# Where the product steps stand among the attention slots of chunks 2 and 3, and which bank turns chunk 3's x

## The chip, the cores and the metric

The kernel runs on one core of one Trainium2 chip. The metric is the device time of one execution in microseconds (us). The engines are named as the profile names them: PE (TensorE) multiplies matrices, PEld is its loading of weights, ACT (ScalarE) applies functions, DVE (VectorE) does elementwise work, POOL (GpSimd) and SP (SyncE) here mainly issue transfers.

## The reference

An attention layer over 4 batches, 8 heads, 768 positions and 64 numbers per head is followed by a two-layer network. Three heads look back over everything, five only at the first 4 positions (the sinks) and the last 64.

```python
scores = q @ k.T / sqrt(64)                    # [4, 8, 768, 768]
keep   = causal if head in (0, 2, 6) else causal & (pos_k < 4 or 0 <= pos_q - pos_k < 64)
a      = softmax(where(keep, scores, -1e9))
x      = (a @ v).transpose(0, 2, 1, 3).reshape(3072, 512)
h      = x @ w_in                              # [3072, 2048]
out    = maximum(0.01 * h, h) @ w_out          # [3072, 512]
```

## The kernel before

**Chunks.** The 3072 rows are cut into eight chunks of 384. `ORDER` runs them as (batch 0, first half), (batch 1, first half), (batch 0, second half), (batch 1, second half), then the same for batches 2 and 3. Chunks 2 and 3 are thus second halves and need six blocks of keys each.

**Attention of a chunk** (`Attention`) is a list of *slots*, made by `slots(lag=3)`. A *unit* is one group of scores and the values that belong to it: five groups for each of the three full heads, one for each of the five windowed heads, and one group for the sinks, 21 units. Slot t issues the scores of unit t (`qk`, L329, for windowed heads L364, for the sinks L309) into a PSUM bank named `psS`, with the exponential on ScalarE behind it (L334, L369, L312) and, where needed, a mask on VectorE (L337, L339, L373). In the same slot come the value matmuls of unit t - 3 (`do_av`, L298, into `po`). Where a pair of heads is complete, `finish` (L395, L397) adds the sinks' values, takes the reciprocal of the sums and writes `xs`. Three slots later `x_t` turns `xs` with three small matmuls against the identity (L407) and copies the result into `xt`, on ScalarE (L409) or on VectorE (L411). Chunks 2 and 3 so have 21 + 3 + 3 = 27 slots: slots 0 to 20 issue scores, slots 21 to 23 only values, slots 24 and 25 nothing, slot 26 the turn of the last pair. From chunk 4 on, `cross` is set, and the turn is a DMA transpose instead.

**The network of a chunk** has two products. Product 1 (`in_slots`, L563) is 16 steps of four 384-column matmuls into a bank `ph`, each with its activation on ScalarE (L565). Product 2 (`out_slots`, L589) is 16 steps, 48 matmuls of 512 columns, into a bank `py`; the steps hold two to four matmuls each. Each third of a chunk keeps one `py` bank until its 16 matmuls are done; then VectorE copies it out (L595) and SP stores it (L596).

**Banks.** The eight PSUM banks are split by `BANKS` into two each of `ph`, `psS`, `po` and `py`. A matmul that writes a bank waits until the engine that read its last content has done so.

**Order.** The schedule is by hand (`manual_schedule`): each engine runs its instructions in the order in which the program issues them. `merge(ms, as_)` spreads the slots `as_` evenly ahead of the product steps `ms`. Three places matter:

- While chunk 2's attention runs, the product steps beside it are the last four of chunk 0's product 2 (`o0[12:]`) and the first ten of chunk 1's (`o1[0:10]`): 14 steps, 42 matmuls, among 27 slots. Then come `spreads(3)` (VectorE copies chunk 3's turned keys into `kt`, L237).
- In the loop at n = 2, chunk 3's attention stands among chunk 2's product 1 and the rest of chunk 1's product 2, 22 steps in all. Chunk 4's key copies (`spreads(4)`, eight of them) go with the slots from the 17th on.
- At the end of n = 2, the last four steps and the last three slots have an order of their own.

Chunk 2's x is turned in a bank `ph` and copied by ScalarE (`xt_tag="ph"`); chunk 3's is turned in a bank `psS`, the default, and copied by VectorE (`xt_eng="v"`).

Of the kernel before, what the change touches and what calls it, by code (L numbers as in the profile page):

```python
# [21 lines left out]
def kernel(  # L22
# [84 lines left out]
    def load_qk(n, nms="kq"):  # L107
        b, c = ORDER[n]
        for nm in nms:
            t = rot.tile([128, 3, H, D], BF16, name=f"{nm}b", tag=f"{nm}b", bufs=1)  # L110
            raw[nm, n] = t
            for g in range(3):
                nc.gpsimd.dma_start(out=t[:, g], in_=nat[nm][b, c, :, :, g])  # L113

    def load_v(n, gs=range(3)):
        b, c = ORDER[n]
        for g in gs:
            nc.gpsimd.dma_start(out=va[b][:, 3 * c + g, :, 0:D], in_=nat["v"][b, c, :, :, g])  # L118
# [3 lines left out]
    def load_sinks(b, eng=None):  # L122
        vsf[b] = rot.tile([32, D], FP32, name="vsf", tag="vsf", bufs=2)
        (eng or nc.sync).dma_start(out=vsf[b][:], in_=v[b, :, 0:NS, :])

    def sink_values(b, eng):
        n = H - 1
        eng.tensor_tensor(
            vs[b % 2][0:32, 1:H, 0:D],
            vsf[b].rearrange("p (o d) -> p o d", o=1).to_broadcast([32, n, D]),  # L130
            m_sink[0:32, 1:H].rearrange("p (h o) -> p h o", o=1).to_broadcast([32, n, D]),
            op=ALU.mult)
# [8 lines left out]
    def v_shift(n, eng=None):  # L141
        eng = eng or nc.sync
        i, c = ORDER[n]
        lo, hi = (0, 2) if c == 0 else (2, 5)
        eng.dma_start(out=vb[i][0:64, lo:hi], in_=va[i][64:128, lo:hi])
        eng.dma_start(out=vb[i][64:128, lo:hi], in_=va[i][0:64, lo + 1 : hi + 1])
# [77 lines left out]
    def turn_dma(n):  # L224
        qx[n] = rot.tile([128, 3, 4, 128], BF16, name="qd", tag="qd", bufs=3)
        raw["kx", n] = rot.tile([128, 3, 4, 128], BF16, name="kd", tag="kd", bufs=2)
        for nm, dst in (("k", raw["kx", n]), ("q", qx[n])):
            nc.sync.dma_start_transpose(out=dst.rearrange("p g q t -> p (g q) t"),
                                        in_=raw[nm, n].rearrange("p g h d -> p (g h d)"))

    def spreads(n):
        b, c = ORDER[n]

        def spread(g, hh):
            r = slice(64 * hh, 64 * hh + 64)
            o = CH * c + 128 * g
            nc.vector.tensor_copy(kt[b % 2][hh][r, :, o : o + 128], raw["kx", n][r, g])  # L237

        r = [lambda g=g, hh=hh: spread(g, hh) for g in range(3) for hh in range(2)]
        if c == 0:  # L240
            r += sink_keys_by(b)
        return r
# [4 lines left out]
    def into(slots, extra):  # L247
        r, extra = [], list(extra)
        for j, s in enumerate(slots):
            r.append(s)  # L250
            if 5 * j >= 2 * len(slots) and extra:
                r.append(extra.pop(0))
                if len(extra) > len(slots) - j - 2:
                    r.append(extra.pop(0))
        return r + extra
# [299 lines left out]
    py = {}  # L555

    def in_slots(n, tags=("ph",)):
        def tick(t):
            if n not in gs:
                gs[n] = rot.tile([128, NG, CH], BF16, name="g", tag="g", bufs=2)  # L560
            ph = bank(tags[t % len(tags)], [128, 512], FP32)
            for g in range(KG):
                nc.tensor.matmul(ph[:, 0:CH], lhsT=w_in_bf[:, g, 128 * t : 128 * t + 128],  # L563
                                 rhs=xts[n][:, g, :] if n else xts[0][:, :, g, :], start=(g == 0), stop=(g == KG - 1))
            nc.scalar.activation(out=gs[n][:, t, :], in_=ph[:, 0:CH], func=ACTF.Prelu, alpha=0.01)  # L565

        return [lambda t=t: tick(t) for t in range(NG)]
# [14 lines left out]
    def out_slots(n, tags=("py", "py", "py"), halves=False):  # L582
        slots = []

        def part(tt, lo, hi, tag, c0, c1):
            if lo == 0:
                py[n] = bank(tag, [128, 512], FP32)
            for ng in range(lo, hi):
                nc.tensor.matmul(py[n][:, 0 : c1 - c0], lhsT=gs[n][:, ng, 128 * tt : 128 * tt + 128],  # L589
                                 rhs=w_out_bf[:, ng, c0:c1], start=(ng == 0), stop=(ng == NG - 1))  # L590
            if hi == NG:
                o = rot.tile([128, DM], FP32, name="o", tag="o", bufs=6)
                b, c = ORDER[n]
                r0 = S * b + CH * c + 128 * tt
                nc.vector.tensor_copy(o[:, 0 : c1 - c0], py[n][:, 0 : c1 - c0])  # L595
                nc.sync.dma_start(out=out[r0 : r0 + 128, c0:c1], in_=o[:, 0 : c1 - c0])  # L596

        for tt in range(3):
            if halves and tt == 2:
                slots.append(lambda: part(2, 0, NG, "py", 0, 256))  # L600
                slots.append(lambda: part(2, 0, NG, "psS", 256, 384))
                slots.append(lambda: part(2, 0, NG, "po", 384, 512))
                continue
            lo = 0
            for w in ([3, 3, 3, 3, 4], [3, 3, 3, 3, 4], [3, 3, 3, 3, 2, 2])[tt]:
                slots.append(lambda tt=tt, lo=lo, w=w: part(tt, lo, lo + w, tags[tt], 0, DM))
                lo += w
        return slots

    def run(*lists):  # L610
        for l in lists:
            for f in l:
                f()

    def both(s, e):
        return lambda: (s(), e and e())

    def merge(ms, as_):

        r, done = [], 0  # L620
        for j, m in enumerate(ms):
            want = (j + 1) * len(as_) // len(ms)
            r += as_[done:want] + [m]
            done = want
        return r + as_[done:]
# [152 lines left out]
    o0, o1 = out_slots(0), out_slots(1)  # L778
# [1 line left out]
    run(spreads(2))  # L780
    run(o0[6:12])
    v_shift(3)
    run(merge(o0[12:] + o1[0:10], Attention(2, xt_tag="ph").slots(lag=3)))
    run(spreads(3))
    outs = o1[10:]

    for n in range(2, NCH):
        a, extra = [], ()
        if n + 2 < NCH:
            turn_dma(n + 2)  # L790
            v_shift(n + 2)
            extra = spreads(n + 2)
            if ORDER[n + 2][1] == 0:
                load_sinks(ORDER[n + 2][0], nc.gpsimd)
                sink_values(ORDER[n + 2][0], nc.gpsimd)
            if n + 3 < NCH:
                load_qk(n + 3)
                load_v(n + 3)
        if n + 1 < NCH:
            a = Attention(n + 1, xt_eng="v", cross=n > 2).slots(lag=2 if n > 2 else 3)  # L800
            a = into(a, extra) if n > 2 else a
        ms = merge(in_slots(n), outs)
        rest = ms[-9:] if a and n > 2 else []
        if n == 2:
            a, rest = [both(s, e) for s, e in zip(a[:-3], [None] * 16 + extra)], [ms[-4], a[-3], ms[-3], a[-2], a[-1], ms[-2], ms[-1]]
            ms = ms[:-4] + rest
        run(merge(ms[: len(ms) - len(rest)], a), rest)
        outs = out_slots(n) if n + 1 < NCH else out_slots(n, ("psS", "psS", "py"), True)
    run(outs)
# [35 lines left out]
```

## Time and profile before

| What | Value |
|---|---|
| Runs | 234.07, 233.84, 235.79, 234.61 us |
| Median | 234.34 us |
| The profiled execution, its own time | 234.07 us |
| Its span in the trace | 232.3 us |
| PE busy | 224.9 us (97%) |
| ACT busy | 127.8 us (55%) |
| DVE busy | 98.3 us (42%) |
| POOL busy | 71.2 us (31%) |
| Granted PE clock, mean | 1.00 |

The span runs from the first instruction to the end of the last; the time of the execution is 1.8 us more. A row of a timeline gives the start in us from the span's start, the length, the engine, the line of the kernel, what it writes and reads, the shape, how many were merged into the row, and in brackets the idle time before it with what ended it. The length of a matmul in these rows holds its way through the array, which overlaps with the next one, so the pace of matmuls is read from the differences of their starts.

### The profile page before, as it was taken

Reading aid. Unit: us, or ns where it says so; the run is one execution under the profiler, and the core shown is the slowest. Engines: PE = TensorE matmul, PEld = TensorE weight load, DVE = VectorE, ACT = ScalarE, POOL = GpSimd, SP = SyncE. Lnnn points to the kernel's source line nnn. Section 1 sums busy time; section 2 is a strip of 40 time slices with the busy share of each in tenths; the row PEclk is TensorE's granted clock in tenths of the full one; section 3 lists DMA queues with packets and bytes.
Section 4 is the critical chain, followed back from the end, with each engine's and each line's share of the span. In section 5 each row is a group of like instructions: output and inputs, shape, how many; then the busy total and the mean of one; then the engine's idle time right before and its main releaser. Section 6 shows DMA issues by size and latency. Waiting matters only on the chain.

```text
span 232.3 us, 5117 instructions
## 1 busy us (share of the span) xinstructions
PE 224.9 (97%) x2080; PEld 139.2 (60%) x2080; DVE 98.3 (42%) x282; ACT 127.8 (55%) x275; POOL 71.2 (31%) x87
## 2 busy tenths in 40 slices
PE   7899999999999999999999999999999999999994
PEld 4687865545655666656566655666555665555554
DVE  7797475042556278367224541245213341111121
ACT  5767856705756875654365536766366764343300
POOL 8996635048068088185006700000000000000000
PEclk9999999999999999999999999999999999999999
DMA  9999999999999999999959992921210220111112
GB/s 132 166 164 181 205 207 164 179 155 173 160 224 202 177 177 143 150 165 169 134 104 176 179 159 65 185 65 34 65 45 0 65 80 20 45 45 45 48 45 92
DMA packets 109480, 28.98 MB, mean 125 GB/s; under 512 B 101248, under 2 KB 105744, under 8 KB 109456
## 3 DMA queue, kind: packets, MB, share of 16 engines
q0 software_dynamic: 77088, 13.39, 76.9%
q1 hardware_dynamic: 31312, 15.00, 30.7%
q10 hardware_dynamic: 1056, 0.26, 0.5%
q8 instruction: 16, 0.26, 0.5%
q14 instruction: 8, 0.07, 0.1%
HBM read 27.30 MB, written 6.29 MB: 145 GB/s over the span
## 4 chain that ended last, share of the span: by engine, by line
PE 86%; POOL 5%; DMA 4%; DVE 3%; issue 0%; ACT 0%; POOLq 0%
PE py L589 31%; PE ph L563 30%; PE po L298 7%; PE psS L329 5%; DMA w_in_bf<-in_moe_w_in_dram 4%; PE psS L589 3%; PE psS L364 3%; PE psS L563 2%; PE psS L309 2%; PE ph L576 1%; POOL kb L113 1%; POOL va L118 1%; POOL qb L113 1%; DVE kt L237 1%; POOL k L104 1%; POOL q L105 1%
## 5 line engine op out<-in xcount | busy, mean ns | idle before, releaser
L589 PE MATMUL py<-w_out_bf,g 128*128 128x512 bf16 (+1 forms) x352 | 90.9, 374 | 0.0
L563 PE MATMUL ph<-xt,w_in_bf 128*128 128x384 bf16 x448 | 90.4, 326 | 0.0
L565 ACT ACTIVATE g<-ph 128x384 bf16<-128x384 f32 x112 | 54.9, 490 | 57.5 <-PE ph L563 56.5
L563 PEld LDWEIGHTS <-w_in_bf 128*128 128x128 bf16 x480 | 44.1, 98 | 31.3
L589 PEld LDWEIGHTS <-g 128*128 128x128 bf16 x416 | 35.9, 98 | 25.8
L334 ACT ACTIVATE at<-psS 128x384 bf16<-128x384 f32 x78 | 36.9, 489 | 18.7 <-PE psS L329 18.5
L595 DVE COPY o<-py 128x512 f32<-128x512 f32 (+1 forms) x22 | 14.9, 679 | 51.3 <-PE py L589 51.0
L113 POOL DMA_DIRECT2D kb<-in_k_dram x21 | 18.7, 908 | 37.6 <-DMA kd<-kb 36.5
L329 PE MATMUL psS<-qd,kt 128*128 128x384 bf16 (+2 forms) x90 | 23.0, 294 | 0.5 <-ACT at L334 0.3
L118 POOL DMA_DIRECT2D va<-in_v_dram x24 | 21.6, 930 | 2.2 <-DMA w_out_bf<-in_moe_w_out_dram 1.8
L113 POOL DMA_DIRECT2D qb<-in_q_dram x21 | 18.6, 915 | 5.7 <-DMA w_in_bf<-in_moe_w_in_dram 1.8
L298 PE MATMUL po<-va,at 128*128 128x65 bf16 x228 | 19.2, 193 | 0.0
L369 ACT ACTIVATE ats<-psS 128x384 bf16<-128x384 f32 x35 | 16.7, 488 | 3.6 <-PE psS L364 3.1
L373 DVE TENSOR_TENSOR ats<-ats,m_win 128x384 bf16<-128x384 bf16 x35 | 12.7, 365 | 14.3 <-ACT ats L369 13.8
L298 PEld LDWEIGHTS <-at 128*128 128x128 bf16 x234 | 14.8, 98 | 4.8 <-issue 0.2
L397 DVE TENSOR_TENSOR xs<-po,linv 128x384 bf16<-128x384 f32 x27 | 15.0, 557 | 0.9
L237 DVE COPY kt<-kd 64x512 bf16<-64x512 bf16 x36 | 14.6, 404 | 0.6
L329 PEld LDWEIGHTS <-kt 128*128 128x128 bf16 x99 | 9.4, 97 | 8.1 <-issue 0.9
L364 PEld LDWEIGHTS <-kt 128*128 128x128 bf16 x210 | 10.6, 98 | 5.4
L339 DVE TENSOR_TENSOR at<-at,m_caus 128x128 bf16<-128x128 bf16 x21 | 4.7, 223 | 21.0 <-ACT at L334 20.8
L298 PEld LDWEIGHTS <-ats 128*128 128x128 bf16 x210 | 10.4, 97 | 4.0 <-DVE xs L397 0.4
L395 DVE RECIPROCAL linv<-po 128x6 f32<-128x6 f32 x27 | 5.2, 193 | 16.1 <-PE po L298 16.0
(143 smaller groups left out, 205.2 us busy)
## 6 DMA issues: line engine op xcount, KB each, us to landing
out_dram<-o SPq DMA_DIRECT2D x23, 256.0 KB, 2.3
va<-in_v_dram POOLq DMA_DIRECT2D x24, 128.0 KB, 7.6
kb<-in_k_dram POOLq DMA_DIRECT2D x21, 128.0 KB, 5.5
qb<-in_q_dram POOLq DMA_DIRECT2D x21, 128.0 KB, 6.2
w_in_bf<-in_moe_w_in_dram POOLq DMA_DIRECT2D x4, 512.0 KB, 8.9
w_out_bf<-in_moe_w_out_dram POOLq DMA_DIRECT2D x4, 512.0 KB, 14.0
vb<-va SPq DMA_DIRECT2D x8, 195.0 KB, 4.0
vb<-va SPq DMA_DIRECT2D x4, 130.0 KB, 3.7
```

The lines of the kernel that those rows point to most:

```text
L113: nc.gpsimd.dma_start(out=t[:, g], in_=nat[nm][b, c, :, :, g])
L118: nc.gpsimd.dma_start(out=va[b][:, 3 * c + g, :, 0:D], in_=nat["v"][b, c, :, :, g])
L237: nc.vector.tensor_copy(kt[b % 2][hh][r, :, o : o + 128], raw["kx", n][r, g])
L298: nc.tensor.matmul(o, lhsT=lhsT, rhs=rhs, start=first, stop=False, skip_group_check=True)
L329: nc.tensor.matmul(s[:, off : off + w], lhsT=kt[i][hh][:, p, 128 * kj : 128 * kj + 128], rhs=q_of(n, p, lo, CH), start=(j == 0), stop=(j = ...
L334: nc.scalar.activation(out=a[:, 0:off], in_=s[:, 0:off], func=ACTF.Exp, scale=SM)
L364: nc.tensor.matmul(s[:, 64 * m : 64 * m + 64], lhsT=kt[i][hh][:, p, k0 : k0 + 128], rhs=q_of(n, p, 64 * m, 64 * m + 64), start=(m == 0), s ...
L369: nc.scalar.activation(out=av_, in_=s[:, 0:CH].rearrange("p (j e f) -> p j e f", j=3, e=2), func=ACTF.Exp, scale=SM)
L397: nc.vector.tensor_tensor(xs[:], po[:, :, :, 0:D], linv.to_broadcast([128, 3, 2, D]), op=ALU.mult)
L563: nc.tensor.matmul(ph[:, 0:CH], lhsT=w_in_bf[:, g, 128 * t : 128 * t + 128], rhs=xts[n][:, g, :] if n else xts[0][:, :, g, :], start=(g == ...
L565: nc.scalar.activation(out=gs[n][:, t, :], in_=ph[:, 0:CH], func=ACTF.Prelu, alpha=0.01)
L589: nc.tensor.matmul(py[n][:, 0 : c1 - c0], lhsT=gs[n][:, ng, 128 * tt : 128 * tt + 128], rhs=w_out_bf[:, ng, c0:c1], start=(ng == 0), stop= ...
```

## The change

The diff in full:

```diff
@@ -611,6 +611,10 @@
         for l in lists:
             for f in l:
                 f()
+
+    def tail(ms, a):
+
+        return [a[0], ms[0], a[1], ms[1], a[2], ms[2], ms[3], *a[3:]]
 
     def both(s, e):
         return lambda: (s(), e and e())
@@ -780,7 +784,8 @@
     run(spreads(2))
     run(o0[6:12])
     v_shift(3)
-    run(merge(o0[12:] + o1[0:10], Attention(2, xt_tag="ph").slots(lag=3)))
+    a2, m2 = Attention(2, xt_tag="ph").slots(lag=3), o0[12:] + o1[0:10]
+    run(merge(m2[:10], a2[:12]), tail(m2[10:], a2[12:]))
     run(spreads(3))
     outs = o1[10:]
 
@@ -797,13 +802,14 @@
                 load_qk(n + 3)
                 load_v(n + 3)
         if n + 1 < NCH:
-            a = Attention(n + 1, xt_eng="v", cross=n > 2).slots(lag=2 if n > 2 else 3)
+            a = Attention(n + 1, xt_eng="v", xt_tag="py", cross=n > 2).slots(lag=2 if n > 2 else 3)
             a = into(a, extra) if n > 2 else a
         ms = merge(in_slots(n), outs)
         rest = ms[-9:] if a and n > 2 else []
         if n == 2:
-            a, rest = [both(s, e) for s, e in zip(a[:-3], [None] * 16 + extra)], [ms[-4], a[-3], ms[-3], a[-2], a[-1], ms[-2], ms[-1]]
-            ms = ms[:-4] + rest
+            a = [both(s, e) for s, e in zip(a, [None] * 16 + extra + [None] * 3)]
+            rest = tail(ms[-6:-2], a[-6:]) + ms[-2:]
+            ms, a = ms[:-6] + rest, a[:-6]
         run(merge(ms[: len(ms) - len(rest)], a), rest)
         outs = out_slots(n) if n + 1 < NCH else out_slots(n, ("psS", "psS", "py"), True)
     run(outs)
```

It has three parts. First, chunk 2's attention: the first ten product steps are merged with the first 12 slots, and the last four steps with the other 15 slots by `tail`, which alternates three slots with three steps, puts the fourth step after the third, and then the remaining slots. Second, chunk 3's attention: 16 steps are merged with the first 21 slots, and the last six slots and six steps follow by `tail` and two steps at the end. Third, chunk 3's x is turned in a bank `py` instead of `psS`. No instruction is added or removed on any engine.

## The prediction

> **What bounds the kernel now.** I read the page first (busy shares, slices, chain), then the timelines of TensorE, VectorE and ScalarE through the stages that the change touches.
>
> ```profile
> PE 224.9 (97%) x2080; PEld 139.2 (60%) x2080; DVE 98.3 (42%) x282; ACT 127.8 (55%) x275; POOL 71.2 (31%) x87
> ...
> PEclk9999999999999999999999999999999999999999
> ...
> PE 86%; POOL 5%; DMA 4%; DVE 3%; issue 0%; ACT 0%; POOLq 0%
> ```
>
> TensorE is the bound, in work and not only in busy share: three L589 matmuls start within 0.65 us (0.216 each), four L563 ones also within 0.65 (0.162 each), with nothing between. A new order can gain only holes. Start-to-start times less this streaming leave these from 53.8 to 100 us (TensorE's timeline: start, us, line, tiles, count, [idle]):
>
> ```profile
> 68.59 0.26 PE L298 MATMUL po<-vs,at_sink 128*128 128x65 bf16 x3
> 68.68 0.81 PE L589 MATMUL py<-w_out_bf,g 128*128 128x512 bf16 x3
> 69.73 0.34 PE L407 MATMUL ph<-ident,xs 128*128 128x128 bf16 x3 [0.24 <-DVE xs L397]
> 69.91 1.03 PE L589 MATMUL py<-w_out_bf,g 128*128 128x512 bf16 x4
> 70.77 0.33 PE L329 MATMUL psS<-qd,kt 128*128 128x384 bf16 x1
> ...
> 72.39 0.63 PE L329 MATMUL psS<-qd,kt 128*128 128x384 bf16 x2
> ...
> 73.61 0.64 PE L329 MATMUL psS<-qd,kt 128*128 128x256 bf16 x2
> ...
> 86.93 0.33 PE L329 MATMUL psS<-qd,kt 128*128 128x256 bf16 x2 [0.32 <-ACT at L334]
> ```
>
> - **Chunk 2's last x:** sinks start at 68.59, the turn at 69.73, 1.14 later; 0.09 of sinks and 0.65 of product lie between, so 0.40 is lost.
> - **Chunk 3's first scores:** two pairs take 0.63 and 0.64 where 0.49 and 0.33 would do: 0.15 lost (two adjacent scores, two banks) and 0.30 (the second matmul waits for keys).
> - **Chunk 3's x turned in psS:** the score at 86.93 stands 0.49 late: the turn at 86.28 took a score bank. Another 0.08 goes at 80.79.
>
> Together 1.42 us: even a perfect change gains only that. VectorE's timeline at the first two:
>
> ```profile
> 68.88 0.20 DVE L395 RECIPROCAL linv<-po 128x6 f32<-128x6 f32 x1 [1.02 <-PE po L298]
> 69.11 0.56 DVE L397 TENSOR_TENSOR xs<-po,linv 128x384 bf16<-128x384 f32 x1
> 70.97 0.69 DVE L595 COPY o<-py 128x512 f32<-128x512 f32 x1 [1.30 <-PE py L589]
> 71.58 2.70 DVE L237 COPY kt<-kd 64x512 bf16<-64x512 bf16 x6
> ```
>
> From sinks to turn: 0.29 to the reciprocal, 0.23 to the product, 0.62 to the turn. The six key copies stand behind the output copy that waits for the last product step. ScalarE's timeline gives the pace of scores:
>
> ```profile
> 62.21 0.87 ACT L369 ACTIVATE ats<-psS 128x384 bf16<-128x384 f32 x2
> ...
> 70.11 0.49 ACT L409 ACTIVATE xt<-ph 128x384 bf16<-128x384 bf16 x1 [2.25 <-PE ph L407]
> 71.13 0.49 ACT L334 ACTIVATE at<-psS 128x384 bf16<-128x384 f32 x1 [0.54 <-PE psS L329]
> ```
>
> ScalarE starts 0.36 after a score starts (70.77 to 71.13), takes 0.49, and follows itself at 0.385 (two in 0.87). A bank is free 0.05 after: the score at 86.93 follows the exponential of 86.39 to 86.88.
>
> **Part 1, chunk 2's order.** No instruction is added or removed; 42 product matmuls stand among 27 slots before and after. But the written tail takes one step each after slots 12 and 13, two after slot 14, then slots 15 to 26 bare (the list has 15 slots, not six). Six of these issue scores; the last x gets no cover. In bare slots TensorE needs 0.163 for scores, 0.092 for three value matmuls (six: 0.186), 0.09 for sinks (0.17 for pair 2), 0.165 for a turn. With 0 at slot 15's score, ScalarE idle and the last output copy on VectorE from 0.20:
>
> - s15 at 0; exponential 0.36 to 0.85. s16 at 0.44; 0.80 to 1.29.
> - s17 could go at 0.79; its bank is free at 0.90: **0.11** lost. Exponential 1.26 to 1.75. s18 at 1.42; 1.78 to 2.27.
> - Slot 18's values need the po bank that pair 1's xs frees. Output copy at 0.20, reciprocal at 0.81 (row pitch 0.61), xs 1.03, free 1.65 instead of 1.58: **0.07**.
> - Turn 1 at 1.74, its ScalarE copy at 2.16; s19 at 1.91, exponential 2.55 to 3.04.
> - s20 could go at 2.17, bank free at 2.32: **0.15**. Exponential 2.94 to 3.43. Turn 2 at 2.59; slot 21's values end at 2.84.
> - Slot 22's values need exponential 19 and its mask (0.04 wait, 0.29, 0.06): 3.43, **0.59** lost. Slot 23's need exponential 20 and mask (0.36): 3.89 against 3.52, **0.37**.
> - Sinks at 4.07; turn at 4.07 + 1.14 = 5.21 against 4.16: **1.05**.
> - Chunk 3's first score at 5.37, L563 from 5.54; its fourth matmul needs this x, copied by ScalarE from 5.59 to 6.08: 6.14 against 6.02, **0.12**.
>
> Sum 2.46 lost; before 0.40 there (and 0.06 at 55.9, gone). **Net +2.0 us.** Output copies and stores also move, earlier: SP's and POOL's lists are the same item for item, and SP's transposes for chunk 4 (74.89) wait for loads, so nothing follows there.
>
> [...]
>
> **Part 2, start of chunk 3.** A product step goes between its third and fourth score: that bank wait (0.15) goes, about 0.05 stays at the fifth (ScalarE is behind by one copy). The key copies no longer wait for an output copy: they begin 0.15 before the turn, and the fifth ends some 2.4 later, at 7.3, while its reader stands at 5.37 + 2.9 = 8.3. The 0.30 goes. **-0.40.**
>
> **Part 3, chunk 3's x in py.** Product 2's running tile keeps one py bank; all four turns share the other. The 0.08 and 0.49 go. New waits: turn 2 waits for turn 1's VectorE copy. The before copy ended 1.22 after its turn (86.28 to 87.50), ready at 1.28; in the new order turn 2 stands 1.34 after turn 1: it fits by 0.06. Behind a late turn 2 stand an L563 step and the last values, and ScalarE waits for that step; if the cover fails, some 0.2 to 0.5 is lost. The next product tile needs turn 3's copy: 0.78 after the turn (row before), against 1.25 of work. Last, two product matmuls now stand before slot 23's values, not after, so the last turn has 1.30 of L563 behind its sinks; with VectorE still at key copies it will be about 0.10 late. **-0.45.** Bounds: -0.57 and +0.1. I take the value by the row of that copy.
>
> **Sum.** +2.0 - 0.40 - 0.45 = **+1.15 us**. Everything behind is TensorE work at the same pace, with one other hole (0.31 at 163.7), so the delay reaches the end. Profiled execution: 234.07 (span 232.3) becomes 235.2. The median of the runs is 234.34, 0.27 above; on it 235.5. I give **235.3**, 0.4% up; a measurement of this kernel tells about 1% from no change, so this is "within 1%".
>
> **Rivals.**
> 1. *The bare stretch costs little.* If scores run far enough ahead, only the last x's hole grows: 1.05 + 0.12 - 0.46 - 0.85 = -0.1: **233.9 to 234.2**. For it: the waits list shows only 0.3 us of TensorE waiting for ScalarE before. Against it: that is with product steps between; the rows' 0.36 + 0.49 and two banks leave no lead. 10%.
> 2. *The shared py bank stalls chunk 3.* VectorE's key copies took 0.43 to 0.62 there, and turns 2 and 3 wait behind them. Part 3 turns from -0.45 to about +0.2: **235.9**. 10%.
> 3. *The clock drops (slower by over 1%).* From 2.8 to 5.2 TensorE does 0.45 of work. [...] My longest hole is 1.05 and the granted clock is 1.00 in the rows with holes up to 0.5[...]. [...] No row shows such a stretch. 8%.
> 4. *All stalls vanish and none comes*: 1.42 off, 232.7. The order contradicts it. 1%.
>
> **Chances.** The sum 71%, rival 1 10%, rival 2 10%, rival 3 8%, rival 4 1%. The sum's own error (part 1 by 0.7, runs by 0.4) puts a few of its cases over +2.3 us: slower 0.11; faster 0.01; within 1% 0.88. The range takes in rivals 1 and 2 and the edge of 3: 233.9 to 236.7.
>
> **What would show it.** Right: a turn in ph with over 0.8 us idle before it, behind VectorE's xs; two value groups late by 0.3 to 0.6 behind masks; scores of chunk 3 with no wait for ScalarE at its third x; key copies done before chunk 3's fifth score; clock 1.00. Wrong: TensorE without idle in chunk 2's last ten slots; turns in py waiting over 0.2; a granted clock under 1.

## The result

The changed kernel takes 236.59 us (median of 43 runs, 234.53 to 238.36) against 234.40 before (64 runs). The ratio is 1.0068, 95% interval 1.0053 to 1.0083: 1.6 us slower, within 1%. (The ratio leaves out the four runs of the changed kernel that lie over 1.5% above its fastest; the medians of all runs are 0.9% apart.) The forecast was 235.3, with a range of 233.9 to 236.7, so the median lies only 0.1 us under the upper end.

The runs fall into two groups. In 30 of 44 (the profiled one included) the mean granted clock is 0.998 to 1.000, and their median is 235.7 us, 1.3 above before. In the other 14 it is 0.991 to 0.993, and their median is 237.8. The profiled execution belongs to the first group: 236.93 us, span 235.2. Its page, busy time, slices and chain:

```profile
PE 226.1 (96%) x2080; PEld 139.6 (59%) x2080; DVE 97.0 (41%) x282; ACT 127.9 (54%) x275; POOL 71.3 (30%) x87
...
PE   8788999999997999999999999999999999999994
...
PEclk9999999999999999999999999999999999999999
...
PE 85%; POOL 5%; DMA 4%; DVE 2%; ACT 1%; issue 0%; POOLq 0%
```

The thirteenth slice of PE (70.6 to 76.4 us) now shows a 7. Its span is 2.9 us longer than before's, but part of that has nothing to do with the change. TensorE's waits (total, times, longest) begin with a transfer at the start of the run, 1.3 us here against 0.3 before:

```profile
PE psS L203 <- DMA kb<-in_k_dram: 1.3, 3, 0.6
...
PE ph L407 <- DVE xs L397: 0.9, 1, 0.9
```

The first scores of chunk 2 stand at 55.34 instead of 53.86, for the most part for that reason. In three more profiles of the changed kernel they stand at 54.31, 54.05 and 55.42, and the spans are 233.6, 233.6 and 234.7; so this is the run, not the order.

From there on, holes (start to start, less the streaming time) are 2.98 us up to 100 us, against 1.48 before; 0.13 of them lie ahead of those first scores and have nothing to do with the change. The three other profiles have 2.6, 2.8 and 2.5. TensorE's timeline in the bare slots:

```profile
69.65 0.32 PE L329 MATMUL psS<-qd,kt 128*128 128x384 bf16 x1
...
71.07 0.34 PE L364 MATMUL psS<-qd,kt 128*128 128x64 bf16 x6
...
71.50 0.26 PE L298 MATMUL po<-va,at 128*128 128x65 bf16 x3
72.16 0.27 PE L298 MATMUL po<-va,at 128*128 128x65 bf16 x3 [0.41 <-DVE at L337]
72.61 0.20 PE L298 MATMUL po<-vb,ats 128*128 128x65 bf16 x1 [0.18 <-DVE ats L373]
...
72.81 0.26 PE L298 MATMUL po<-vs,at_sink 128*128 128x65 bf16 x3
73.95 0.34 PE L407 MATMUL ph<-ident,xs 128*128 128x128 bf16 x3 [0.88 <-DVE xs L397]
74.12 0.33 PE L329 MATMUL psS<-qd,kt 128*128 128x384 bf16 x1
74.29 0.90 PE L563 MATMUL ph<-xt,w_in_bf 128*128 128x384 bf16 x4
...
76.65 0.33 PE L329 MATMUL psS<-qd,kt 128*128 128x384 bf16 x1
...
76.96 0.33 PE L329 MATMUL psS<-qd,kt 128*128 128x256 bf16 x2
```

The hole ahead of 73.95 is the one that stood at 69.73 before, grown from 0.40 to 1.05; sinks to turn is 1.14 again. The holes ahead of 72.16 and 72.61 (0.57 and 0.35) are values that wait for the masks of slots 19 and 20, and these for ScalarE, which was paced first by the banks and then by itself:

```profile
69.11 1.90 ACT L334 ACTIVATE at<-psS 128x384 bf16<-128x384 f32 x4 [1.27 <-PE psS L329]
70.91 0.48 ACT L409 ACTIVATE xt<-ph 128x384 bf16<-128x384 bf16 x1
71.28 0.50 ACT L334 ACTIVATE at<-psS 128x384 bf16<-128x384 f32 x1
71.65 0.51 ACT L369 ACTIVATE ats<-psS 128x384 bf16<-128x384 f32 x1
72.02 0.53 ACT L409 ACTIVATE xt<-ph 128x384 bf16<-128x384 bf16 x1
```

Eight activations close upon each other: slots 15 to 18, turn 1, slots 19 and 20, turn 2. The first four take 0.45 each, as the banks allow (69.11 to 70.91), the next three 0.37. The two pairs of scores that cost 0.45 before now cost 0.06: the second matmul at 76.96 no longer waits for keys.

In chunk 3, the score after turn 1 has no hole (90.05, after 0.65 of L563), but the last turn has one:

```profile
89.24 0.33 PE L407 MATMUL py<-ident,xs 128*128 128x128 bf16 x3
89.40 0.81 PE L563 MATMUL ph<-xt,w_in_bf 128*128 128x384 bf16 x4
90.05 0.33 PE L329 MATMUL psS<-qd,kt 128*128 128x256 bf16 x2
...
94.61 0.34 PE L407 MATMUL py<-ident,xs 128*128 128x128 bf16 x3 [0.22 <-DVE ksink L266]
```

VectorE's timeline says why. Key copies stand ahead of slot 20's mask (L373, at 92.14) and between it and the reciprocal:

```profile
91.48 0.63 DVE L237 COPY kt<-kd 64x512 bf16<-64x512 bf16 x1
...
92.69 0.60 DVE L237 COPY kt<-kd 64x512 bf16<-64x512 bf16 x2
93.20 0.53 DVE L262 COPY ksink<-kt 64x16 bf16<-64x16 bf16 x1
93.77 0.20 DVE L395 RECIPROCAL linv<-po 128x6 f32<-128x6 f32 x1
94.00 0.56 DVE L397 TENSOR_TENSOR xs<-po,linv 128x384 bf16<-128x384 f32 x1
```

The hole is 0.38. No single copy explains it: the small one of 16 columns took 0.53 us here and 0.15 before, but with the two copies ahead of it the time is the same (92.69 to 93.77 here, 89.48 to 90.58 before: 1.08 and 1.10). What varies is the sum of these copies with the one at 91.48. From that copy to the reciprocal it is 2.29 us here, and 1.91, 2.20 and 1.97 in the three other profiles of the changed kernel, where the hole is 0, 0.29 and 0.06. Why the copies vary is not shown.

### The profile page after: what moved, and what is told of

Read it like the earlier page. It is cut to its first block, busy times and chain, and to the rows that moved or that the text cites. A ratio compares the mean times of both kernels' runs of the same rounds, so it can differ in the third digit from the quotient of the medians.

```text
span 235.2 us, 5117 instructions
## 1 busy us (share of the span) xinstructions
PE 226.1 (96%) x2080; PEld 139.6 (59%) x2080; DVE 97.0 (41%) x282; ACT 127.9 (54%) x275; POOL 71.3 (30%) x87
## 4 chain that ended last, share of the span: by engine, by line
PE 85%; POOL 5%; DMA 4%; DVE 2%; ACT 1%; issue 0%; POOLq 0%
PE py L589 32%; PE ph L563 30%; PE po L298 6%; PE psS L329 5%; DMA w_in_bf<-in_moe_w_in_dram 4%; PE psS L589 3%; PE psS L364 3%; PE psS L563 2%; PE psS L309 2%; PE ph L576 1%; POOL kb L113 1%; POOL va L118 1%; POOL qb L113 1%; DVE xs L397 1%; ACT at L334 1%; POOL k L104 1%
## 5 line engine op out<-in xcount | busy, mean ns | idle before, releaser
L589 PE MATMUL py<-w_out_bf,g 128*128 128x512 bf16 (+1 forms) x352 | 90.7, 374 | 0.0
L563 PE MATMUL ph<-xt,w_in_bf 128*128 128x384 bf16 x448 | 90.4, 326 | 0.0
L563 PEld LDWEIGHTS <-w_in_bf 128*128 128x128 bf16 x480 | 44.0, 98 | 31.0
L589 PEld LDWEIGHTS <-g 128*128 128x128 bf16 x416 | 36.0, 98 | 26.3
L373 DVE TENSOR_TENSOR ats<-ats,m_win 128x384 bf16<-128x384 bf16 x35 | 12.4, 357 | 14.4 <-ACT ats L369 14.0
L237 DVE COPY kt<-kd 64x512 bf16<-64x512 bf16 x36 | 12.7, 354 | 0.9 <-DMA kd<-kb 0.3
```

## The experiments

The theory: chunk 2's bare slots are the loss, chunk 3's part a small gain. Rivals: chunk 3's turns in py cost the time; the order of chunk 2 as such costs it; and, for the runs at a clock of 0.993, that idle time in the bare slots lowers the clock, against a cause that lies elsewhere.

**Chunk 2's order undone.**

```diff
-    run(merge(m2[:10], a2[:12]), tail(m2[10:], a2[12:]))
+    run(merge(m2, a2))
```

> Chunk 2's slots and product steps stand as before; chunk 3's order and its x in py are as after. Theory (the bare slots are the loss): the 2.4 us of holes in chunk 2's end fall back to 0.46, the key copies stand behind the output copy again (0.36 lost at chunk 3's fifth score), the last turn of chunk 3 keeps its 0.38: holes of 1.2 us from 53 to 100 against 1.48 before, so 0.3 us faster than before (ratio 0.9988) and no run with a granted clock of 0.993. Rival (chunk 3's part is what costs): slower than before by 0.5 us or more. Rival (the clock drop has nothing to do with the bare slots): about a third of the runs still show 0.993.

Measured: ratio 0.9992 to before (0.997 to 1.0015), median 234.81 against 235.18. The last turn of chunk 2 waits as before:

```profile
71.22 0.34 PE L407 MATMUL ph<-ident,xs 128*128 128x128 bf16 x3 [0.24 <-DVE xs L397]
```

Holes in its trace: 0.46 in chunk 2 (0.40 of them ahead of this turn), 0.42 at chunk 3's fifth score, 0.47 at chunk 3's last turn. Without the bare slots the loss is gone, so chunk 3's part does not cost 0.5 us. The small gain lies inside the interval. Two of 14 runs stand at 0.991 and 0.992: this fall of the clock occurs without bare slots too.

**Chunk 2's order alone.**

Against the changed kernel ("..." marks lines left out):

```diff
-            a = Attention(n + 1, xt_eng="v", xt_tag="py", cross=n > 2).slots(lag=2 if n > 2 else 3)
+            a = Attention(n + 1, xt_eng="v", cross=n > 2).slots(lag=2 if n > 2 else 3)
...
-            a = [both(s, e) for s, e in zip(a, [None] * 16 + extra + [None] * 3)]
-            rest = tail(ms[-6:-2], a[-6:]) + ms[-2:]
-            ms, a = ms[:-6] + rest, a[:-6]
+            a, rest = [both(s, e) for s, e in zip(a[:-3], [None] * 16 + extra)], [ms[-4], a[-3], ms[-3], a[-2], a[-1], ms[-2], ms[-1]]
+            ms = ms[:-4] + rest
```

> Only chunk 2's order is the new one; chunk 3's end and its x in psS are as before. Theory: the bare slots cost their 2.4 us, the key copies are early (no 0.30), chunk 3 loses its 0.15, 0.08 and 0.49 again: holes of 3.1 us, 1.7 us slower than before in runs at full clock, and a third of the runs at 0.993, about 2 us longer still. Rival (chunk 3's part costs): no more than 0.5 us slower than before.

Measured: 1.0072 (1.0045 to 1.0099), 1.7 us. The last turn of chunk 2 waits as in the changed kernel:

```profile
72.60 0.34 PE L407 MATMUL ph<-ident,xs 128*128 128x128 bf16 x3 [0.88 <-DVE xs L397]
```

The trace holds the seven holes of the bare slots (2.4 in all), 0.15 at two adjacent scores of chunk 3, 0.08 and 0.48 at its turns in psS. The sum is confirmed. None of eight runs had a lower clock, which the theory of the clock had expected of a third.

**The bare slots filled.**

```diff
+    for j, w in ((22, 3), (23, 2), (24, 8)):
+        a2[j] = (lambda s, w: lambda: (idle("py", w), s()))(a2[j], w)
     run(merge(m2[:10], a2[:12]), tail(m2[10:], a2[12:]))
```

> After, plus 13 matmuls of 256 columns on zeros that nobody reads, into a free py bank: 3 ahead of slot 22's values, 2 ahead of slot 23's, 8 ahead of the last turn. They need 0.32, 0.22 and 0.87 us and stand in holes of 0.57, 0.35 and 1.05. Theory[...]: the times of the runs at full clock stay as after (235 to 237), no run shows 0.993, and the median is lower than that of after by 0.7 us or so. Rival (the clock drops for another reason): a third of the runs at 0.993 as in after. Rival (fillers delay the real work): full-clock runs longer by up to 1.4 us.

Measured: 1.0039 (1.0021 to 1.0056), and one run of 22 at 0.993. The holes of 0.57, 0.35 and 1.05 shrink to 0.25, 0.13 and 0.17 and no real work is later, so the fillers are free. On the clock this comparison says nothing: the two kernels with the bare slots left empty that ran on the same chip (chunk 2's order alone, above, and the next one) have no low run in 14 either.

**Chunk 3's x in psS, in the new order.**

```diff
-            a = Attention(n + 1, xt_eng="v", xt_tag="py", cross=n > 2).slots(lag=2 if n > 2 else 3)
+            a = Attention(n + 1, xt_eng="v", cross=n > 2).slots(lag=2 if n > 2 else 3)
```

> After with chunk 3's x turned in psS again, everything else as after. Theory (the bank is what took the 0.49 and 0.08 away): slot 20's scores wait for the copy of turn 1 (0.2) and turn 2 for the exponential of slot 19 (0.4), turn 0 0.08; 0.5 to 0.7 us slower than after at the same clock. Rival (the new order alone is enough, a product step now stands between turn 1 and the next score): no difference from after.

Measured: 1.0093 (1.0066 to 1.012), about 0.9 us over the changed kernel (1.0056 in the comparison below, on another chip; the two intervals overlap a little, so the traces are the better evidence). TensorE's timeline has two turns that wait for a score bank:

```profile
84.03 0.33 PE L407 MATMUL psS<-ident,xs 128*128 128x128 bf16 x3 [0.44 <-ACT at L334]
...
91.46 0.33 PE L407 MATMUL psS<-ident,xs 128*128 128x128 bf16 x3 [0.30 <-ACT at L334]
```

Start to start these holes are 0.60 and 0.46, and slot 20's scores lose 0.14. That is 1.20 in all, where psS cost 0.57 before the change. The bank is what helps; the new order without it would be worse than the old. Turn 0 at 0.60 had been expected at 0.08: it stands right behind two adjacent scores here.

**The changed kernel again, beside the next three.**

> The changed kernel once more, beside before and the next three on one chip. Theory (holes of 2.98 us against 1.48, from the two traces): 1.3 to 1.6 us slower than before in runs at full clock (ratio 1.0055 to 1.007). Theory[...]: about a third of the runs at a granted clock of 0.993 and some 2 us longer. Rival (the clock drop is a matter of the chip or of the start of the run): as few such runs as before shows.

Measured: 1.0056 (1.0035 to 1.0077); 17 of 22 runs at full clock with a median of 235.65, and five at 0.993 with a median of 237.2. Three of 53 runs of before stood at 0.991 to 0.993 on that chip.

**The tail given six slots.**

```diff
-    run(merge(m2[:10], a2[:12]), tail(m2[10:], a2[12:]))
+    run(merge(m2[:10], a2[:-6]), tail(m2[10:], a2[-6:]))
```

> After with the tail given chunk 2's last six slots instead of its last 15, as in chunk 3. Theory (bare slots are the loss): ten product steps stand among slots 0 to 20, four between slots 21 and 23 and the turn; the sinks have 1.5 us of product behind them against 1.14 needed, so the last turn waits for nothing; key copies again stand behind the output copy (0.2 to 0.35 at chunk 3's fifth score), chunk 3's last turn 0.1 to 0.45. Holes of 0.3 to 0.9 us against 1.48: 0.6 to 1.2 us faster than before. Rival (the loss is in the new order of chunk 2 as such, scores going first): slower than before.

Measured: 0.998 (0.996 to 1.0), median 234.14 against 234.70. The last turn of chunk 2 starts as its cover ends:

```profile
69.58 1.67 PE L589 MATMUL py<-w_out_bf,g 128*128 128x512 bf16 x7
71.09 0.33 PE L407 MATMUL ph<-ident,xs 128*128 128x128 bf16 x3
```

Holes: 0.15 and 0.23 at adjacent scores of chunk 2, 0.09 where L563 waits for the last x, 0.06 at chunk 3's fifth score, 0.30 at its last turn. So the same helper, given six slots instead of fifteen, turns 1.3 us lost (1.0056 in the same comparison) into about 0.5 gained, at the edge of the interval; scores first is not the cause. The gain falls just short of the forecast of 0.6 to 1.2, because adjacent scores opened two holes that I had not counted.

**The tail of six, and key copies out of the way.**

Against the kernel with the tail of six:

```diff
-    run(merge(m2[:10], a2[:-6]), tail(m2[10:], a2[-6:]))
-    run(spreads(3))
+    s3 = spreads(3)
+    run(merge(m2[:10], a2[:-6]), [a2[21], m2[10], *s3[:2], a2[22], m2[11], *s3[2:4], a2[23], m2[12], *s3[4:], m2[13], *a2[24:]])
...
-            a = [both(s, e) for s, e in zip(a, [None] * 16 + extra + [None] * 3)]
-            rest = tail(ms[-6:-2], a[-6:]) + ms[-2:]
+            a = [both(s, e) for s, e in zip(a, [None] * 16 + extra[:4] + [None] * 4 + extra[4:6] + [None])]
+            rest = tail(ms[-6:-2], a[-6:]) + [extra[6], ms[-2], extra[7], ms[-1]]
```

> As the kernel with the tail of six, and the key copies of chunk 3 go two each after the first two tail steps and before the last one, ahead of the output copy; of chunk 4's eight key copies, two go after chunk 3's last xs and the two small ones after the last turn. Theory: the fifth score's 0.3 and chunk 3's last 0.1 to 0.45 go too: holes of 0.1 to 0.4 us, 1.1 to 1.4 us faster than before (ratio 0.994 to 0.9955). Rival (VectorE is full there and the copies only delay xs): no faster than before.

Measured: 0.9956 (0.993 to 0.9983), 233.63 against 234.70. This beats both kernels; the gain of 1.0 us is just under the forecast of 1.1 to 1.4. TensorE's timeline at the two last turns (chunk 2 at 70.77, chunk 3 at 91.05):

```profile
69.26 1.67 PE L589 MATMUL py<-w_out_bf,g 128*128 128x512 bf16 x7
70.77 0.33 PE L407 MATMUL ph<-ident,xs 128*128 128x128 bf16 x3
```

```profile
89.75 1.46 PE L563 MATMUL ph<-xt,w_in_bf 128*128 128x384 bf16 x8
91.05 0.33 PE L407 MATMUL py<-ident,xs 128*128 128x128 bf16 x3
```

Both turns start as their cover ends, 1.51 us of product and 1.30 of L563.

**A longer hole.** The six key copies go ahead of pair 3's reciprocal.

```diff
+    a2[23] = (lambda s: lambda: (spread_keys(3), s()))(a2[23])
     run(merge(m2[:10], a2[:12]), tail(m2[10:], a2[12:]))
-    run(spreads(3))
```

> After with the six key copies of chunk 3 run ahead of pair 3's reciprocal and xs, so that the last turn waits about 2.2 us longer: a hole of some 3.2 us instead of 1.05. By the holes alone 2.2 us slower than after. Theory[...]: half or more of the runs at a granted clock of 0.993, each 1.7 to 2 us longer still. Rival (the clock drop comes from elsewhere): no more such runs than after shows on this chip.

Measured: 1.0201 (1.0163 to 1.024), 239.88 us; all six runs between 0.984 and 0.993. TensorE's timeline:

```profile
71.91 0.26 PE L298 MATMUL po<-va,at 128*128 128x65 bf16 x3 [0.41 <-DVE at L337]
72.36 0.20 PE L298 MATMUL po<-vb,ats 128*128 128x65 bf16 x1 [0.19 <-DVE ats L373]
...
72.56 0.26 PE L298 MATMUL po<-vs,at_sink 128*128 128x65 bf16 x3
75.73 0.50 PE L407 MATMUL ph<-ident,xs 128*128 128x128 bf16 x3 [2.92 <-DVE xs L397]
76.02 0.53 PE L329 MATMUL psS<-qd,kt 128*128 128x384 bf16 x1
76.34 1.49 PE L563 MATMUL ph<-xt,w_in_bf 128*128 128x384 bf16 x4
77.62 0.53 PE L329 MATMUL psS<-qd,kt 128*128 128x384 bf16 x1
```

The hole is 3.08 us. After it four L563 matmuls need 1.28 us (76.34 to 77.62) instead of 0.65. Windows of the same trace (window, length, busy time of each engine, granted clock, DMA, GB/s):

```profile
70.00:73.50 3.50, 2.21 (x41) 1.62 (x38) 2.77 (x10) 2.27 (x6) 3.50 (x5) 1.00 1.35 277
73.50:77.00 3.50, 1.27 (x7) 0.77 (x8) 2.08 (x5) 0.73 (x2) 3.50 (x5) 0.52 2.12 196
77.00:80.50 3.50, 3.50 (x12) 1.60 (x11) 0.00 (x0) 1.88 (x5) 0.08 (x1) 0.50 2.43 154
80.50:84.00 3.50, 3.50 (x39) 2.33 (x38) 0.88 (x3) 2.65 (x6) 0.55 (x1) 1.00 1.52 182
```

The granted clock falls to half inside the hole and stays there for about 7 us; TensorE is busy in 4.8 of them. Shorter windows give the two moments:

```profile
73.60:73.80 0.20, 0.00 (x0) 0.00 (x0) 0.20 (x1) 0.00 (x0) 0.20 (x1) 0.64 1.87 228
80.40:80.60 0.20, 0.20 (x2) 0.14 (x1) 0.00 (x0) 0.00 (x0) 0.00 (x0) 0.79 2.46 157
```

Between 1.00 and 0.50, a mean of 0.64 puts the fall at 73.66 and one of 0.79 the rise at 80.48, 6.83 us later. At 73.66 the long hole was only 1.0 us old (the sinks' three matmuls are through at 72.65, by their pace), and in the changed kernel, 1.14 after its sinks, the turn would have come at 73.70. By the brackets of the rows, TensorE's idle time from 71.50 up to the fall is 0.41, 0.19 and 0.85 us (72.81 to 73.66); the changed kernel's rows have 0.41, 0.18 and 0.88 there. So up to the fall TensorE had seen no more than the bare slots of the changed kernel, and in this run the clock fell on no more idle time than these give.

**A hole of middle size.** Two of the six key copies go ahead of that reciprocal, for a hole between 1.05 and 3.08 us: if more idle time lowers the clock in more runs, the share of low runs should lie between as well.

```diff
-    run(merge(m2[:10], a2[:12]), tail(m2[10:], a2[12:]))
-    run(spreads(3))
+    s3 = spreads(3)
+    a2[23] = (lambda s: lambda: (run(s3[:2]), s()))(a2[23])
+    run(merge(m2[:10], a2[:12]), tail(m2[10:], a2[12:]), s3[2:])
```

> After with two of chunk 3's six key copies ahead of pair 3's reciprocal: the last turn's hole grows from 1.05 to about 1.7 us (two copies at 0.29 to 0.45). By the holes alone 0.7 us slower than after, some 2.1 slower than before. Theory[...]: between the changed kernel (19 of 80 runs of kernels with the bare stretch at 0.991 to 0.993) and the hole of 3.1 us (6 of 6): about half of the runs. Rival[...]: a quarter or fewer.

Measured: 1.0137 (1.0097 to 1.0177). The hole did not grow: in the changed kernel VectorE stands idle for 0.55 us ahead of that reciprocal, and the two copies fitted in; the trace shows 1.05 as in the changed kernel. So the dose was not varied. This is one more run of the same holes, and four of its six runs are at 0.993 (237.7 to 238.6) and two at full clock (236.0 and 236.1).

**The longer hole filled.** Against the kernel with the longer hole:

```diff
     a2[23] = (lambda s: lambda: (spread_keys(3), s()))(a2[23])
+    a2[24] = (lambda s: lambda: (idle("py", 26), s()))(a2[24])
```

> As the kernel with the hole of 3.1 us before the last turn, with 26 matmuls of 256 columns on zeros that nobody reads issued into it (2.8 us). The real work is as late as there: by the holes 2.0 to 2.2 us slower than after at full clock, some 3.6 slower than before. Theory (idle TensorE, not lateness, halves the clock): no run under 0.99, at most one in ten at 0.993, and the time about 1.2 to 3 us below that of the kernel with the empty hole (239.9). Rival (something else in that order lowers the clock): the same clock and time as there.

Measured: 1.0144 (1.0114 to 1.0174), 237.71 us; all six runs at 0.999 or 1.000. The windows of the same stretch:

```profile
70.00:73.50 3.50, 2.90 (x46) 2.43 (x44) 2.82 (x9) 1.60 (x5) 3.50 (x5) 1.00 1.64 254
73.50:77.00 3.50, 3.50 (x29) 2.43 (x27) 1.13 (x4) 1.81 (x5) 2.34 (x3) 1.00 2.24 169
77.00:80.50 3.50, 3.50 (x38) 2.31 (x36) 0.87 (x3) 3.01 (x8) 0.00 (x0) 1.00 2.47 164
```

From sinks to turn it is 2.94 us here (71.86 to 74.80) against 3.17 with the empty hole (72.56 to 75.73), so the real work is nearly as late, yet the kernel is 2.2 us faster (2.0 against the runs of before beside each). The idle time, not the lateness, lowers the clock: 0.999 or 1.000 here, 0.984 to 0.993 with the empty hole. The two ran on different chips, but on the chip of this one the kernel with the empty hole of 1.05 us had four low runs of six, so the chip does not explain it. TensorE's timeline shows the fillers:

```profile
71.86 0.26 PE L298 MATMUL po<-vs,at_sink 128*128 128x65 bf16 x3
71.96 3.00 PE L151 MATMUL py<-blank 128*128 128x256 bf16 x26
74.80 0.33 PE L407 MATMUL ph<-ident,xs 128*128 128x128 bf16 x3
```

**Where the clock falls in the changed kernel itself.**

> One more profile of the changed kernel, to see where its clock falls in a run at 0.993. Theory: in about one look of four the granted clock is 0.5 for one stretch[...] that begins within or right behind the bare slots (some 71 to 76 us). Rival: it falls at the start of the run, where TensorE also waits.

> The same once more: about one in four to catch the fall of the clock, at 71 to 76 us by the theory, in the first 20 us by the rival.

Both runs were at full clock (235.32 and 236.49 us), so neither could show it.

Counted over the runs of these comparisons and of the result: kernels with the bare slots and the 1.05 us hole stand at 0.991 to 0.993 in 23 of 88 runs (14 of 44, 5 of 22, 0 of 8, 0 of 6, 4 of 6, 0 of 2); kernels without bare slots in 8 of 153 (before 4 of 101, then 2 of 14, 1 of 22, 1 of 16); bare slots with fillers 1 of 22.

The counts follow the holes in chunk 2's end, as far as the traces give them: 0.4 to 0.5 us in all in before, with chunk 2's order undone and with the tail of six; 2.4 with the bare slots as they are; some 4.4 with the long hole (six of six), an estimate with 3.08 in place of 1.05 in 2.41. With fillers the three largest shrink from 1.97 to 0.55 (one of 22). Why only some runs of one program fall is not shown. The few low runs of kernels without bare slots may come from the start, where TensorE stands idle for 1.1 us at one place (L151 behind `blank`) in the traces of before and of the changed kernel; that is not shown either.

## Why the prediction was right, and which steps were off

- **What bounds it.** Right. TensorE's streaming pace is the same before and after (0.216 us from start to start for a matmul of L589, whose own row has 0.38, and 0.162 for one of L563), and at a granted clock of 1.00 only holes changed.
- **Part 1, the bare slots.** Right in place and size, and not by luck: 2.46 us summed, 2.41 in the trace, hole by hole 0.13, 0.07, 0.15, 0.57, 0.35, 1.05, 0.09 against 0.11, 0.07, 0.15, 0.59, 0.37, 1.05, 0.12. Chunk 2's order alone (+1.7 us) and chunk 2's order undone (no loss) confirm that it is the cause.
- **ScalarE's pace.** Right within 0.02: turn 1's copy to turn 2's copy is three steps in 1.11 us (70.91 to 72.02), 0.37 each, against the 0.385 taken from the rows of before.
- **Part 2, chunk 3's start.** Right: 0.45 became 0.06, for -0.40 forecast.
- **Part 3, x in py.** The bank was the right reason: with psS in the new order the turns cost 1.20. The last turn is the loose term: 0.10 forecast, 0.38 in the profiled run, 0 to 0.29 in the three other profiles of the changed kernel (0.18 on average) and up to 0.47 in other kernels with this end. The wait was the right one (VectorE at key copies), but the time of these copies varies from run to run. So part 3 gave -0.2 to -0.57, not a fixed -0.45. One of the prediction's own signs of being wrong, a turn in py waiting over 0.2, came true in two of the four profiles.
- **Sum at full clock.** 1.15 us forecast; the holes say 1.4 in the profiled run and 1.0 to 1.3 in the three others, the 30 runs at full clock 1.3 (235.7 against 234.4). That is within 0.2 us, with one term 0.1 to 0.3 off either way.
- **Rival 3, the clock.** This is the step that was off in weight. I gave 8% to a drop of the clock instead of the sum. The weight was an estimate of mine that no row showed: before's granted clock is 1.00 in every window from 0 to 220 us, and its holes there, up to 0.5 in the stages of the change, say nothing of a stretch with holes of 0.57, 0.35 and 1.05 close together. The drop came on top of the sum, in a part of the runs: 14 of 44, 2.1 us each, some 0.7 us on the mean, so the sign of a granted clock under 1 came true as well. That the median of all runs still lies in the range, by 0.1 us, is partly luck: it hangs on how many runs fell. The small holes stand close together: from 71.6 to 73.9 three holes leave 1.97 us idle. (The prediction has 0.45 us of work there; its own holes leave 0.36, the trace 0.39.) That idle time at this place lowers the clock is shown by the filled and the empty long hole (0.999 or 1.000 against 0.984 to 0.993, six runs each); that the bare slots alone suffice, by the moment of the fall in one trace, 73.66, 0.04 us before the changed kernel's turn would have come. No profile caught one of the 14 falls themselves. Why two kernels with the same holes had none in 14 runs stays open: at the rate of the others (23 of 74) chance would do that in about one of 200 cases, and they ran on another chip than the runs at 5 of 22 and 4 of 6, but no run tests the chip.
- **Rivals 1 and 2.** Rival 1 fell: the bare stretch cost its full sum. Rival 2 was half right: the late copy was not turn 1's but the last xs.

## What to carry to other kernels

Where the matrix engine is the bound, price a new order by its holes: list each engine's pace in the stretch from rows (here 0.36 + 0.49 + 0.05 us per bank, 0.385 per activation, 1.14 from sums to turn) and lay the instructions on it one by one; in the bare slots each hole came out within 0.03 us of the trace. Cover for a wait is worth its place, not its amount: four product steps given to the end of 27 slots cost 1.3 us at full clock when they stood ahead of the waits and gained 0.5 when they stood in them. Several small holes close together (0.57, 0.35 and 1.05 us between 71.6 and 73.9 here) can cost more than their sum: in 23 of 88 runs with them the mean granted clock was 0.991 to 0.993, and in the one fall that a trace shows ahead of the run's end it went to half for 6.83 us when the last hole was only 1.0 us old. Matmuls that nobody reads, a little shorter than the hole (0.87 us in 1.05), cost no time; that they keep the clock up is shown for the long hole (0.999 or 1.000 in six runs), not for the small ones.

## What the hardware showed that I had not expected

- With a hole of 3.08 us behind the small ones, the mean granted clock was under 1 in six of six runs (0.984 to 0.993), and with that hole filled by 26 dummy matmuls it was 0.999 or 1.000 in six of six. In the one trace of such a fall the half clock (0.50) lasted 6.83 us, and the kernel with the empty hole took 2.2 us longer.
- That fall came 1.0 us into the hole, after idle times of 0.41, 0.19 and 0.85 us by the brackets, no more than the changed kernel's 0.41, 0.18 and 0.88: in this run the full 3.08 us were not needed.
- In kernels whose longest hole was 1.05 us, some runs stood at a mean clock of 0.991 to 0.993 and were 1.6 to 2.1 us longer; how many differed from 0 of 8 to 4 of 6 between kernels with the same holes there.
- 13 matmuls of 256 columns put into holes that were a little longer than they cost no time: the turn behind them stood 1.14 us after the sinks, as without them.
